# Query projection from SBUF, a reordered query block and paced W2 loads in a one-core transformer layer

## The chip, the core and the metric

The kernel runs on one core of a Trainium2 chip. A core has a matrix engine (PE, with its weight loads listed apart as PEld), a vector engine (DVE), a scalar engine for activations (ACT), a general engine (POOL) and a queue engine that issues the DMA transfers (SP). They run side by side and wait for each other through semaphores. SBUF is the on-chip working memory, PSUM the eight banks that PE writes its sums to, and DRAM the memory off the core. The metric is the device time of one execution in microseconds (us), the median of several runs; less is better.

## The reference

One pre-norm transformer layer on 2048 tokens of width 1024, in bf16: 32 heads of 32 channels, full (not causal) softmax attention, and an MLP of width 3584 with the tanh form of GELU.

```python
def _A_ref(x, wqkv, wo):
    qkv = (x @ wqkv).reshape(B, S, 3, H, Dh).transpose(2, 0, 3, 1, 4)
    q, k, v = qkv[0], qkv[1], qkv[2]
    p = softmax(einsum("bhqd,bhkd->bhqk", q, k) * Dh ** -0.5)
    o = einsum("bhqk,bhkd->bhqd", p, v)
    return o.transpose(0, 2, 1, 3).reshape(B, S, D) @ wo

def _B_ref(x, w1, b1, w2, b2):
    return gelu(x @ w1 + b1) @ w2 + b2          # gelu: tanh form

h  = x + _A_ref(layernorm(x), wqkv, wo)
h2 = h + _B_ref(layernorm(h), w1, b1, w2, b2)
```

## The kernel before, in words

**Tiling.** The 2048 tokens are 16 tiles of 128 (`tt`), four stretches of 512 (`tc`), or eight query blocks of 256 (`qb`, and `u` in the second half of the layer). The 1024 channels are eight groups `g` of four heads. An attention job is one query block and one group: eight rounds, and in each round PE makes the scores of 256 keys for four heads (`qk`, line 796), ACT takes two exponentials of 128 x 1024 (line 807), and PE multiplies them with V (`pv`, line 833) and sums the denominators with a ones matrix (`den`, line 862). There are 64 jobs, and so 1024 exponentials.

**Stages.** At the head, x is loaded, normalised and transposed into `xnT`, four stretches of 512 tokens. Q, K and V of group 0 come first, with the jobs of query blocks 0 to 2 of that group. Then, for g from 1 to 7, `rest_of_projections(g)` makes Q of the first 512 tokens, K of all tokens and V of the next group, and `attention` runs query blocks 0 and 1 of the group (for groups 1 and 2 also block 2). The Q of later tokens goes through DRAM: each result of 128 x 512 is copied out of PSUM by DVE and written to `q_scratch`, and `load_q` fetches 256 columns of it when a job begins. For the second 512 tokens, groups 0, 1 and 2 are projected from `xnT` in SBUF (`proj(0, g, 1, ...)`, through two staging buffers `stg`); the other five groups come later, in `late_q(1, 1, [3..7])`. A `late_q` loads x of its 512 tokens back from a DRAM copy `xd` (1 MB) into one of two buffers `xq`, loads the query weights in blocks of 512 KB into a ring of four, `w1r` (`wblock`), and projects with those. `late_q(2, 0)` and `late_q(3, 1)` do the same for the third and the fourth 512 tokens, for all eight groups.

**Second half.** For a unit `u` of 256 tokens, `wo(u)` is the output projection with the residual, `ln2(u)` the second layer norm followed by two DMA transposes that put the result into `hnT`, `ffn1(u)` 14 blocks of the first MLP matrix, each with a 512 KB load into the ring `w1r`, a bias addition on DVE and, every second block, the tanh on ACT (line 1014), and `ffn2(u, j)` half of the second MLP matrix: seven loads of 512 KB into the ring `w2r` of seven slots, and 56 matmuls of 512 columns. `wo(u)` loads its 2 MB of weights into the same four slots as the ring `w1r`. `wo(u)` needs all eight groups of attention for its query block. The program lists the work as `wo(u+1)`, `ffn2(u,0)`, `ln2(u+1)`, `ffn2(u,1)`, `ffn1(u+1)`, and then attention of query block u+3.

**The order of the work.** Every instruction is a task with its dependencies. `Graph.schedule` (line 109) plans the order for each engine from assumed durations, among them a DMA rate of 280 GB/s with one transfer after the other, and this order is then fixed: an engine waits at the instruction that is next in its list. On PE, `pick_pe` (line 1210) takes `qk` first, `pv` when enough rounds wait, and otherwise the earliest ready piece of the rest, called background here ("bg": projections, `wo`, `ffn1`, `ffn2`). An attention job holds one of the two PSUM banks 6 and 7 while it runs, and background pieces use what is left of these two. SP, the only queue that issues DMAs, takes the ready transfer with the lowest priority number, and of equals the one that the program lists first. A transfer can be given additional tasks that it waits for (`after`).

**Places in SBUF.** The memory of the first half (`ph0`: `xnT` in four stretches of 8 KB per partition, the weight blocks `Wall0`, `1`, `3`, `4`, `5` of 8 KB each, `stg`) is used again in the second half (`ffn`: from its start 8 KB of `hch`; then 18 KB of `gT` and `uu`, with `xq0`, `xq1` and `lq` in the same place; 4 KB of `hnT`; 16 KB of `w1r`; 28 KB of `w2r`; 4 KB). A transfer into the second use waits until the first use has been read for the last time. In the kernel before, `xq0` lies over `xnT` of the second 512 tokens, `xq1` over that of the third, `hch` over the first, and `w1r` over the end of the fourth, `Wall0` and most of `Wall1`.

Of the kernel before, what the change touches and what calls it, by code (L numbers as in the profile page):

```python
# [328 lines left out]
def build_kernel(nc, A_x, A_wqkv, A_wo, B_w1, B_b1, B_w2, B_b2, out):  # L329
# [87 lines left out]
    ffn = Area(top.cur)  # L417


    xnT, B_xnTt = sb(ph0, "xnT", [P, 4, DC, 512], BF, 4, 4)  # L420
    k_hi = Area(B_KT[8 * (G - 2)].lo)
    Wall, B_W = [], []
    for k in range(6):
        h, b = sb(k_hi if k == 2 else ph0, "Wall%d" % k, [P, DC, 512], BF, 1, 4)
        Wall.append(h)
        B_W.append(b)
    assert k_hi.cur <= B_V[0].lo
    NXB = 4
    v_hi = Area(att_hi - 2 * NT * P * 2)
# [225 lines left out]

    def tr_tile(tt, bank, evac, prio=0):
        tc, t4 = divmod(tt, 4)
        transposes(xb[:, tt % NXB, :], B_xb[tt % NXB], bank, xnT[:, tc, :, t4 * P:(t4 + 1) * P], B_xnTt[tc][t4], evac, prio)

    def proj(which, g, tc, bank, evac, direct=False):  # L660

        blk, c = divmod(which * D + g * P, 512)
        o = B_stg[cnt["sg"] % NSG]
        free = o.w + o.r if which == 0 and not direct else []
        for dc in range(DC):
            mm(bank, Wall[blk][:, dc, c:c + P], xnT[:, tc, dc, :], dc == 0, dc == DC - 1,
               [B_W[blk][c // P]] + B_xnTt[tc], True, after=free if dc == 0 else ())
        if which == 1:
            dst, wr = KT[:, g, 512 * tc:512 * tc + 512], B_KT[8 * g + 2 * tc:8 * g + 2 * tc + 2]
        elif direct:  # L670
            n = q_slot(0, g, 2)
            q_slots[1, g] = n + 1
            dst, wr = QT[:, n:n + 2, :].rearrange("p a c -> p (a c)"), B_QT[n:n + 2]
        else:
            s = cnt["sg"] % NSG
            cnt["sg"] += 1
            dst, wr = stg[:, s, :], [B_stg[s]]
        if evac == "act":
            t = act(lambda a: a.activation(dst, psum[:, bi(bank), :], ACT.Copy), 512, reads=[bb(bank)], writes=wr, prio=-1)
        else:  # L680
            t = dve(lambda v: v.tensor_copy(dst, psum[:, bi(bank), :]), c_dve_ps(512), reads=[bb(bank)], writes=wr)
        drop(t, bank)
        if which == 0 and not direct:
            dma(qd[g, tc], dst, P * 1024, reads=wr, writes=[B_qd[g][tc]], prio=0)
# [37 lines left out]
    def proj_v(tt, q, bank, evac, after=()):  # L722
# [3 lines left out]
        for k in range(2):  # L726
            tc, t4 = divmod(tt + k, 4)
            for dc in range(DC):
                mm(bank, xnT[:, tc, dc, t4 * P:(t4 + 1) * P], Wall[blk][:, dc, c:c + 256], dc == 0, dc == DC - 1,
                   B_W[blk][c // P:c // P + 2] + [B_xnTt[tc][t4]], True, cols=(256 * k, 256 * k + 256), after=after)  # L730
        dst = V[:, 2 * q:2 * q + 2, tt:tt + 2, :]
        wr = [B_V[NT * g + tt + k] for g in (2 * q, 2 * q + 1) for k in range(2)]
# [4 lines left out]
    def proj_v1(tt, g, n, bank, evac, c0=0, narrow=False, after=()):  # L737

        for k in range(n):
            tc, t4 = divmod(tt + k, 4)  # L740
            for dc in range(DC):
                mm(bank, xnT[:, tc, dc, t4 * P:(t4 + 1) * P], Wall[4][:, dc, P * g:P * g + P], dc == 0, dc == DC - 1,
                   [B_W[4][g], B_xnTt[tc][t4]], narrow, cols=(c0 + P * k, c0 + P * k + P), after=after)
        dst = V[:, g, tt:tt + n, :]
        wr = [B_V[NT * g + tt + k] for k in range(n)]
# [9 lines left out]
    def proj_half(which, hc, bank, evac):  # L755
# [1 line left out]
        tc, h = divmod(hc, 2)  # L757
        blk = 2 * which
        for dc in range(DC):
            mm(bank, Wall[blk][:, dc, 0:P], xnT[:, tc, dc, 256 * h:256 * h + 256], dc == 0, dc == DC - 1,  # L760
               [B_W[blk][0]] + B_xnTt[tc][2 * h:2 * h + 2], True, cols=(0, 256))
        if which == 1:
            dst, wr = KT[:, 0, 256 * hc:256 * hc + 256], [B_KT[hc]]
# [210 lines left out]
    def ffn1(u, tail=False):  # L974
        R = R2 if tail else R1
        for blk in range(FC // 2):
            s = wblock(R, None, block=blk)
            bank = blk % 6 if tail else slot()
            for f in range(2):
                for dc in range(DC):  # L980
                    mm(bank, R.w1[:, s, dc, f * P:(f + 1) * P], hnT[:, dc, :], dc == 0, dc == DC - 1,
                       [R.B_w1[s]] + B_hnT, not tail, (256 * f, 256 * f + 256))
            evict1(u, 2 * blk, bank, tail)
            if not tail and blk % 2:
                gelu(u, blk // 2)

    biased = []

    def evict1(u, fc, bank, tail):
        g, B_g = gs[u], B_gs[u][fc // 2]  # L990
# [27 lines left out]
    def ffn2(u, j, wide=False, W=None, banks=None):  # L1018
# [3 lines left out]
        ws = []  # L1022
        for q in range(FC // 4):
            s = W.next("w2", W.nw2)
            dma(W.w2[:, s, :, :], w2d[j, q], P * 4096, reads=[B_w2d[j][q]], writes=[W.B_w2[s]], prio=1)
            ws.append(s)
        for t in range(2):
            bank = banks[t] if banks and banks[t] is not None else slot()
# [34 lines left out]
    def lead_norm(hc):  # L1063
# [6 lines left out]
        for tt in tts:  # L1070
            if tt < LEAD_PE:
                tr_tile(tt, slot(), "act" if tt in LEAD_ACT else "dve")
            else:
                tc, t4 = divmod(tt, 4)
                last_t[:] = [dma_transpose(xnT[:, tc, :, t4 * P:(t4 + 1) * P], xb[:, tt % NXB, :], P * 2048, [B_xb[tt % NXB]], [B_xnTt[tc][t4]], -4)]
            if tt + 8 < NT:
                last_x.append(x_tile(tt + 8, -4))
    lead_rounds = []
# [29 lines left out]
    rest_w(WQ, P, 2 * P)  # L1108
    rest_w(WV, P, 4 * P)
    lx = last_t or last_x[-1:]  # L1110
    for tc in range(1, 4):
        dma(xd[tc - 1], xnT[:, tc, :, :], P * 8192, reads=B_xnTt[tc], writes=[B_xd[tc - 1]], prio=1)
    rest_w(WK, 2 * P, 3 * P)
    rest_w(WQ, 2 * P, 3 * P)
    rest_w(WK, 3 * P, 4 * P)
# [37 lines left out]
    for g in range(1, G):  # L1153
# [4 lines left out]
        attention(1, [g])  # L1158
        if g in EXTRA:
            attention(2, [g])  # L1160
    for g in range(1, 2):
        if g not in EXTRA:
            proj(0, g, 1, slot(), "dve")
    block_copies()
    late_q(1, 1, [g for g in range(2, G) if g not in EXTRA])
    wo(0)
    ln2(0)
    late_q(2, 0, range(G))
    late_q(3, 1, range(G))
    ffn1(0)  # L1170
    attention(2, [g for g in range(1, G) if g not in EXTRA])
# [145 lines left out]
```

## Time and profile before

| what | value |
|---|---|
| median of 3 runs | 1081.43 us (1081.03 to 1085.59) |
| the profiled execution's own time | 1080.46 us |
| its span | 1078.7 us |
| ACT busy | 1012.8 us, 94% |
| PE busy | 1041.8 us, 97% |
| DVE busy | 751.5 us, 70% |
| exponentials on ACT | 1024 (992 into `PT`, 32 into `PX`), 924.5 + 31.3 us |
| tanh on ACT | 49, 57.2 us |
| DMA traffic | 196.37 MB, mean 182 GB/s |

Times inside the execution are microseconds from the start of the span. "Busy" is the time in which at least one instruction of the engine runs; matmuls overlap and are counted through their pipeline, so a busy PE is not a PE at its peak. The granted clock (PEclk) is the share of its full rate that the chip let PE run at; 1.00 is full. In a line of the timeline, what stands in brackets is the engine's idle time just before, and what ended it.

### The profile page before, as it was taken

Reading aid. Unit: us, or ns where it says so; the run is one execution under the profiler, and the core shown is the slowest. Engines: PE = TensorE matmul, PEld = TensorE weight load, DVE = VectorE, ACT = ScalarE, POOL = GpSimd, SP = SyncE. Lnnn points to the kernel's source line nnn. Section 1 sums busy time; section 2 is a strip of 40 time slices with the busy share of each in tenths; the row PEclk is TensorE's granted clock in tenths of the full one; section 3 lists DMA queues with packets and bytes.
Section 4 is the critical chain, followed back from the end, with each engine's and each line's share of the span. In section 5 each row is a group of like instructions: output and inputs, shape, how many; then the busy total and the mean of one; then the engine's idle time right before and its main releaser. Section 6 shows DMA issues by size and latency. Waiting matters only on the chain.

```text
span 1078.7 us, 41723 instructions
## 1 busy us (share of the span) xinstructions
PE 1041.8 (97%) x18987; PEld 608.7 (56%) x19044; DVE 751.5 (70%) x1438; ACT 1012.8 (94%) x1116; POOL 43.4 (4%) x110
## 2 busy tenths in 40 slices
PE   8999999998899999999999999999999999899998
PEld 6566555554344754674475457447545744474483
DVE  8766666566586896698499669849966967596401
ACT  4999999999999999999999999999999999999650
POOL 4200000000010001001000100100010001000100
PEclk9999999999899999999999999999999999899999
DMA  8560544438474645744764574476466455866260
GB/s 233 151 184 21 154 137 119 139 119 296 157 188 134 206 172 181 251 167 154 260 221 168 188 247 165 149 258 221 158 210 233 178 192 206 241 230 238 91 242 20
DMA packets 136177, 196.37 MB, mean 182 GB/s; under 512 B 49216, under 2 KB 100288, under 8 KB 133184
## 3 DMA queue, kind: packets, MB, share of 16 engines
q1 hardware_dynamic: 136000, 193.70, 53.8%
q8 instruction: 149, 2.44, 0.9%
q14 instruction: 28, 0.23, 0.1%
HBM read 177.94 MB, written 27.26 MB: 190 GB/s over the span
## 4 chain that ended last, share of the span: by engine, by line
ACT 74%; PE 24%; DVE 2%; issue 1%; POOL 0%; POOLq 0%
ACT PT L807 67%; PE ps L559 6%; PE ps L562 5%; PE ps L556 5%; ACT uu L1014 4%; PE ps L796 3%; ACT PX L807 3%; PE ps L833 2%; PE ps L862 1%; PE ps L1055 1%; DVE PS L848 0%; PE ps L629 0%; ACT xnT L636 0%; DVE hch L957 0%; DVE st L608 0%
## 5 line engine op out<-in xcount | busy, mean ns | idle before, releaser
L807 ACT ACTIVATE PT<-ps 128x1024 bf16<-128x1024 f32 x992 | 924.5, 1116 | 7.4 <-PE ps L796 7.3
L848 DVE TENSOR_TENSOR PS<-PT 128x1024 bf16<-128x1024 bf16 x431 | 286.8, 686 | 125.8 <-ACT PT L807 65.1
L796 PE MATMUL ps<-QT,KT 32*128 32x256 bf16 x4096 | 205.0, 274 | 8.9 <-ACT PT L807 5.7
L833 PE MATMUL ps<-PT,V 128*32 128x256 bf16 x3968 | 175.7, 274 | 3.6 <-ACT PT L807 3.5
L796 PEld LDWEIGHTS ps<-QT,KT 32*128 32x128 bf16 x4096 | 61.0, 92 | 164.6 <-ACT PT L807 145.3
L862 PE MATMUL ps<-PS,ones 128*32 128x256 bf16 x1756 | 122.2, 274 | 3.0 <-DVE PS L848 2.7
L559 PE MATMUL ps<-hnT,a_w1r 128*128 128x256 bf16 x979 | 119.1, 273 | 1.7 <-DVE hch L1037 0.5
L833 PEld LDWEIGHTS ps<-PT,V 128*32 128x32 bf16 x3968 | 101.6, 97 | 33.4 <-ACT PT L807 6.3
L559 PEld LDWEIGHTS ps<-hnT,a_w1r 128*128 128x128 bf16 x979 | 90.1, 98 | 26.7 <-issue 15.7
L556 PE MATMUL ps<-a_w2r,gT 128*32 128x512 bf16 x1380 | 99.8, 381 | 0.4 <-DVE gT L1016 0.3
L559 PE MATMUL ps<-a_w2r,gT 128*128 128x512 bf16 x390 | 96.2, 380 | 2.8 <-issue 1.9
L556 PE MATMUL ps<-hnT,a_w1r 128*32 128x256 bf16 x2356 | 83.4, 276 | 1.4 <-DVE gT L992 1.0
L992 DVE TENSOR_TENSOR gT<-ps,b1f 128x512 bf16<-128x512 f32 x98 | 67.3, 687 | 14.5 <-PE ps L559 8.0
L1037 DVE SCALAR_TENSOR_TENSOR hch<-ps,hch 128x512 bf16<-128x512 f32 x32 | 22.0, 689 | 72.1 <-PE ps L562 47.1
L556 PEld LDWEIGHTS ps<-hnT,a_w1r 128*32 128x32 bf16 x2356 | 58.5, 97 | 15.2 <-issue 11.7
L559 PEld LDWEIGHTS ps<-a_w2r,gT 128*128 128x128 bf16 x411 | 35.3, 98 | 46.9 <-issue 12.5
L862 PEld LDWEIGHTS ps<-PS,ones 128*32 128x32 bf16 x1756 | 46.3, 96 | 25.1 <-DVE PS L848 8.8
L1014 ACT ACTIVATE uu<-uu 128x1024 bf16<-128x1024 bf16 x49 | 57.2, 1168 | 0.0
L559 PE MATMUL ps<-xnT,Wall 128*128 128x512 bf16 (+1 forms) x256 | 54.0, 344 | 2.4 <-issue 1.0
L556 PEld LDWEIGHTS ps<-a_w2r,gT 128*32 128x32 bf16 x1380 | 29.9, 96 | 25.7 <-issue 15.2
L613 POOL CAST mvb<-mv 128x2 bf16<-128x2 f32 (+1 forms) x25 | 5.1, 211 | 976.4 <-DVE mv L610 976.4
L878 DVE STREAM_TRANSPOSE OD<-ps 128x256 f32<-128x256 f32 x64 | 28.6, 447 | 11.5 <-PE ps L833 5.9
(91 smaller groups left out, 1018.4 us busy)
## 6 DMA issues: line engine op xcount, KB each, us to landing
a_w2r<-w_blocks SPq DMA_DIRECT2D x105, 512.0 KB, 5.6
a_w1r<-w_blocks SPq DMA_DIRECT2D x98, 512.0 KB, 3.7
wov<-wo_blocks SPq DMA_DIRECT2D x16, 1024.0 KB, 4.8
w_blocks<-in_B_w_dram SPq DMA_DIRECT2D x28, 512.0 KB, 4.0
b_w1r<-w_blocks SPq DMA_DIRECT2D x14, 512.0 KB, 4.1
a_w1r<-in_A_wqkv_dram SPq DMA_DIRECT2D x11, 512.0 KB, 5.2
Wall<-in_A_wqkv_dram SPq DMA_DIRECT2D x17, 256.0 KB, 4.5
xrb<-in_A_x_dram SPq DMA_DIRECT2D x16, 256.0 KB, 4.7
```

Source lines behind the costliest of these rows:

```text
L556: fns.append(lambda p, j=j: p.matmul(psum[32 * j:32 * j + 32, bi(bank), c0:c1], lhsT[:, 32 * j:32 * j + 32], rhs, start=start, stop=stop, ...
L559: t.whole = lambda p: p.matmul(psum[:, bi(bank), c0:c1], lhsT, rhs, start=start, stop=stop, skip_group_check=True)
L562: t = pe(lambda p: p.matmul(psum[:, bi(bank), c0:c1], lhsT, rhs, start=start, stop=stop), occ, reads=reads, writes=[bb(bank)], mode="full" ...
L796: return p.matmul(psum[:, 2 * us[h // 2] + h % 2, 256 * i:256 * i + 256], KT[32 * h:32 * h + 32, g, k0:k0 + P], QT[32 * h:32 * h + 32, qs, :],
L807: act(lambda a, u=u, k=k: a.activation(PTs[s][:, k, :, :], psum[:, 2 * u:2 * u + 2, :], ACT.Exp, bias=0.0, scale=SCALE), 1024, reads=[B_ps ...
L833: fns.append(lambda p, i=i, h=h: p.matmul(psum[32 * h:32 * h + 32, bi(bank), 0:256], V[:, g, 2 * r + i, 32 * h:32 * h + 32], PTs[s][:, h / ...
L848: dve(lambda v: v.tensor_tensor(PS[:, n, :, :], pairs[:, :, 0:256], pairs[:, :, 256:512], ALU.add), c_dve(1024, 2), reads=B_PTs[s], writes ...
L862: fns.append(lambda p, h=h, rhs=rhs, i=i: p.matmul(psum[32 * h:32 * h + 32, bi(bank), 256:512], ones32[:, :], rhs, start=False, stop=last, ...
L878: t = dve(lambda v: v.transpose(OD[:, o, 1, :], psum[:, bi(bank), 256:512]), 0.36, reads=[self.B_O, self.B_D], writes=B_D, prio=-1)
L992: t = dve(lambda v: v.tensor_tensor(g[:, fc:fc + 2, :], psum[:, bi(bank), :].rearrange("p (f c) -> p f c", f=2), b1f[:, fc:fc + 2].unsquee ...
L1014: act(lambda a: a.activation(w, w, ACT.Tanh, bias=0.0, scale=KT2), 1024, reads=[B_uu[i]], writes=[B_uu[i]], prio=-1)
L1037: drop(dve(lambda v, hs=hs, bank=bank, half=half: v.scalar_tensor_tensor(hch[:, hs, c], psum[:, bi(bank), :], half, hch[:, hs, c], ALU.mul ...
```

## The change

Three things change.

The places in SBUF: `xnT` becomes four tensors, and these and the weight blocks are laid out in the order xnT1, Wall4, xnT0, xnT2, xnT3, Wall3, Wall5, Wall0, Wall1. So xnT1 (the second 512 tokens) lies under `hch`, Wall4 (V of the first four groups) under `xq0`, xnT0 under `xq1`, parts of xnT2, xnT3 and Wall3 under `w1r`, and Wall0 and Wall1 (the query weights) under `w2r`.

The Q work: `late_q(1, 1, [3..7])` is gone. Groups 3 to 7 of the second 512 tokens are projected by `proj(0, g, 1, ...)` from `xnT` and `Wall` in SBUF, after the attention of group 7 in the listing. The DRAM copy of these tokens of x (1 MB) is not written and not read. `late_q(2, 0, range(G))` is listed ahead of `wo(0)` and `ln2(0)`, in place of behind them.

The W2 loads: for j = 0 and u from 0 to 6, load q of `ffn2(u, 0)` waits in addition for the last matmul of block 2q of `ffn1(u)`.

```diff
-    xnT, B_xnTt = sb(ph0, "xnT", [P, 4, DC, 512], BF, 4, 4)
     k_hi = Area(B_KT[8 * (G - 2)].lo)
-    Wall, B_W = [], []
-    for k in range(6):
-        h, b = sb(k_hi if k == 2 else ph0, "Wall%d" % k, [P, DC, 512], BF, 1, 4)
-        Wall.append(h)
-        B_W.append(b)
+    Wall, B_W = [None] * 6, [None] * 6
+    xnT, B_xnTt = [None] * 4, [None] * 4
+    Wall[2], B_W[2] = sb(k_hi, "Wall2", [P, DC, 512], BF, 1, 4)
+    for kind, k in (("x", 1), ("W", 4), ("x", 0), ("x", 2), ("x", 3), ("W", 3), ("W", 5), ("W", 0), ("W", 1)):
+        h, b = sb(ph0, ("xnT%d" if kind == "x" else "Wall%d") % k, [P, DC, 512], BF, 1, 4)
+        if kind == "x":
+            xnT[k], B_xnTt[k] = h, b
+        else:
+            Wall[k], B_W[k] = h, b
...
@@ ffn1
+            blocks1.setdefault(u, []).append(gr.tasks[-1])
             evict1(u, 2 * blk, bank, tail)
...
@@ ffn2
-            dma(W.w2[:, s, :, :], w2d[j, q], P * 4096, reads=[B_w2d[j][q]], writes=[W.B_w2[s]], prio=1)
+            dma(W.w2[:, s, :, :], w2d[j, q], P * 4096, reads=[B_w2d[j][q]], writes=[W.B_w2[s]], prio=1,
+                after=blocks1[u][0 + 2 * q:][:1] if j == 0 and 0 <= u < 7 else ())
...
-    for tc in range(1, 4):
-        dma(xd[tc - 1], xnT[:, tc, :, :], P * 8192, reads=B_xnTt[tc], writes=[B_xd[tc - 1]], prio=1)
+    for tc in range(2, 4):
+        dma(xd[tc - 1], xnT[tc][:, :, :], P * 8192, reads=B_xnTt[tc], writes=[B_xd[tc - 1]], prio=1)
...
-    for g in range(1, 2):
-        if g not in EXTRA:
-            proj(0, g, 1, slot(), "dve")
+    for g in range(3, G):
+        proj(0, g, 1, slot(), "dve")
     block_copies()
-    late_q(1, 1, [g for g in range(2, G) if g not in EXTRA])
+    late_q(2, 0, range(G))
     wo(0)
     ln2(0)
-    late_q(2, 0, range(G))
     late_q(3, 1, range(G))
     ffn1(0)
```

The other lines of the diff only write `xnT[tc][:, ...]` where `xnT[:, tc, ...]` stood.

## The prediction

> **What bounds the kernel now.** I read the page's busy times and slices first, then the chain that ended last, then ACT's timeline for its idle times, and last the table by stretches and the SP queue around these.
>
> ```profile
> PE 1041.8 (97%) x18987; PEld 608.7 (56%) x19044; DVE 751.5 (70%) x1438; ACT 1012.8 (94%) x1116; POOL 43.4 (4%) x110
> ACT  4999999999999999999999999999999999999650
> PEclk9999999999899999999999999999999999899999
> ACT 74%; PE 24%; DVE 2%; issue 1%; POOL 0%; POOLq 0%
> ```
>
> ACT is full from slice 2 to slice 37, and the chain runs over it for 74%. So the time is three pieces: the head to the first exponential at 22.28 us, the exponentials and tanhs to about 1012.2, and the tail to 1078.7, a chain of PE work of the last query block. The change touches neither head nor tail. What it can save is ACT's idle time in the middle, and that is little:
>
> ```profile
> 292.21 11.12 ACT L807 ACTIVATE PT<-ps 128x1024 bf16<-128x1024 f32 x12 [1.55 <-PE ps L796]
> 303.52 16.89 ACT L807 ACTIVATE PT<-ps 128x1024 bf16<-128x1024 f32 x18 [0.19 <-PE ps L796]
> 646.20 2.86 ACT L807 ACTIVATE PT<-ps 128x1024 bf16<-128x1024 f32 x3 [0.47 <-PE ps L796]
> 729.20 8.36 ACT L807 ACTIVATE PT<-ps 128x1024 bf16<-128x1024 f32 x9 [0.22 <-PE ps L796]
> 917.41 2.86 ACT L807 ACTIVATE PT<-ps 128x1024 bf16<-128x1024 f32 x3 [0.37 <-PE ps L796]
> 933.74 8.36 ACT L807 ACTIVATE PT<-ps 128x1024 bf16<-128x1024 f32 x9 [1.50 <-PE ps L796]
> ```
>
> These are all of them: 4.30 us, 0.4% of the time. The two large ones follow stretches in which PE ran short of background. In the table by stretches (first PE, PEld, DVE, ACT and POOL busy; then PEclk, DMA share, GB/s):
>
> ```profile
> 259.00:266.00 7.00, 4.41 (x97) 1.74 (x98) 4.03 (x7) 6.93 (x9) 0.00 (x0) 1.00 0.95 345
> 279.00:289.00 10.00, 6.97 (x153) 3.29 (x154) 5.55 (x12) 10.00 (x12) 0.00 (x0) 0.80 0.81 283
> 289.00:302.00 13.00, 12.98 (x203) 5.88 (x206) 8.45 (x16) 11.45 (x13) 2.23 (x4) 0.89 0.33 96
> 918.00:930.00 12.00, 7.89 (x164) 2.86 (x152) 6.52 (x12) 12.00 (x14) 0.00 (x0) 0.86 0.98 283
> 930.00:934.00 4.00, 4.00 (x84) 2.38 (x80) 0.69 (x1) 2.50 (x4) 0.00 (x0) 0.56 0.23 89
> 1004.00:1011.00 7.00, 4.89 (x117) 2.21 (x110) 3.45 (x6) 6.99 (x8) 0.00 (x0) 1.00 0.10 25
> ```
>
> A lull itself costs ACT nothing, since attention is taken first. It costs when the clock falls (0.80 and 0.86 as means) and the first background burst runs at half rate in front of a score matmul:
>
> ```profile
> 289.02 2.77 PE L559 MATMUL ps<-wov,OT 128*128 128x512 bf16 x6 [0.44 <-DVE OT L893]
> ```
>
> Six matmuls of 512 columns in 2.77 us, where seven take 1.68 us at full clock; ACT's 1.55 us is this. The lulls of 7 us (259 and 1004) left the clock at 1.00.
>
> **Part 1, Q of the second 512 tokens.** Removed: three 512 KB weight blocks, 1 MB of x written and 1 MB read. The 40 matmuls stay, 40 x 0.215 = 8.6 us of PE (0.215 from 54 to 56 matmuls in the tail's 12.03 us), and so do five DVE copies of 0.69 us and five writes of 128 KB. They used to wait for x and weights from 259.9 to 265.9; now both lie in SBUF when K of group 7 ends, near 259, so the 6 us lull goes. It cost ACT nothing (0.07 us busy short), so the gain here is 0; what it gives is that background runs 6 us ahead. Staging: two `stg` buffers, each free when its write has landed (median 3.1 us); behind a project-and-copy of about 3.6 us this can hold a group by 0 to 1.5 us, which the next Q block fills. `hch` now waits for the last of these projections, about 273; it is needed by `wo(0)` at 294 or later.
>
> **Part 2, the third 512 tokens ahead of `wo(0)`.** It moves 64 matmuls (13.8 us of PE), eight copies on DVE, one load of 1 MB, four of 512 KB and eight writes of 128 KB past `wo(0)` (32 matmuls, two loads of 1 MB, two of 256 KB) and past `ln2(0)`, whose POOL work (2.2 us in 289 to 302) and two DMA transposes come later on POOL and SP. Its x can load early, over `Wall4`; its weights wait for K of group 7 and land some 5.2 us behind it, under the Q work. Background gets 0.63 of PE beside attention (8.6 us in 265.9 to 279.6). So it runs from 259 to 259 + 22.4/0.63 = 295, and the lull from 279.6 to 289.0, in which PE waited for the attention output of group 7, is filled. The stall of 1.55 us and the 0.19 us behind it go: -1.74 us (bounds: 0, if a wait of the same size takes its place, since `wo(0)` now waits for its second megabyte, 4.8 us behind the last Q matmul, with 16 matmuls on the first megabyte as cover; and -1.74). `wo(0)` ends near 310 instead of 302.7. Behind it stands the fourth Q block, 13.8/0.63 = 22 us, which hides `ln2(0)` and its transposes.
>
> Together background is about 15 us ahead at `ffn1(0)` (335 instead of 349.8). The units then come every 94.8 us (the loads of `wo` at 383.8, 478.5, 573.2, 668.3, 763.3), against 126 us of exponentials and tanhs each, so background stays bound by PE until it catches up with attention, and that is at unit 6: its last attention output is written at 892.4, and `wo(6)` starts at 892.7.
>
> **Part 3, the W2 loads.** Nothing less is loaded. The seven loads of `ffn2(u,0)` leave the end of `ffn2(u-1,1)` and go out with every second block of `ffn1(u)`, each behind the W1 load that the same matmul frees. Load 6 goes out one block (2.4 us) before `ffn1` ends and lands in 5.6 us; it is read 24 matmuls into `ffn2(u,0)`, 8 us on: hidden. On SP a waiting W2 load holds what is queued behind it, Q loads for attention and W1 loads. At unit 6 it matters most:
>
> ```profile
> 907.92 3.35 SPq L580 DMA_DIRECT2D a_w2r<-w_blocks  x4
> 911.31 3.60 SPq L585 DMA_TRANSPOSE hnT<-a_xb  x1
> 916.56 2.80 SPq L585 DMA_TRANSPOSE hnT<-a_xb  x1
> ```
>
> The transposes go out behind four W2 loads, take 8.7 us to land where those of unit 1 took 2.9, and `ffn1(6)` starts only at 930.2. Without the loads they land about 6 us sooner. But the 12 us of `ffn2(5,1)` that ran behind `wo(6)`, from 906 to 918, will by then be done, for background is 15 us ahead. So the lull stays, from about 902 to 912 instead of 918 to 930, and I leave its 1.50 us where they are (bounds -1.50, and +0.24 by the other such stall, 1.74). The 0.37 us at 917 fell into the load burst and goes; 0.47 and 0.22 us stand 13 and 5 us behind such bursts (622 to 633, 718 to 728), and I take half: together -0.37 - 0.35 = -0.72 us (bounds -1.06, and +1.06 should the loads beside W1 disturb as much as the bursts did).
>
> **What is late next.** If `ffn1(6)` starts 18 us sooner, background ends 18 us sooner, at 986 instead of 1004; the half of `ffn2(6,1)` kept for the tail is bound to a bank that attention holds. Then 986 to 1011 is attention alone, the longest lull of all, and the tail starts at half clock. Recovery took 2.7 us from 289.0 and 3.4 us from 930.2; half of such a stretch of dense PE work is 1.4 to 1.7 us. I take +1.5 (bounds 0, if the clock holds, and +3.4, if twice as long).
>
> Sum: -1.74 - 0.72 + 0 + 1.5 = -0.96 us, on the profiled execution's own 1080.46: 1079.5. The median of the runs lies 0.97 above that execution; I forecast **1079.5 us** and let the range carry that difference.
>
> The Trainium skill, "TensorE: Matmul & The Clock Gate", section "HAM oscillation", puts it as no PE gap above some 3.4 us. By that rule no lull here would throttle: attention never leaves PE idle for more than 1.42 us. The trace disagrees (0.80 and 0.86 with gaps of at most 1.42 us), so I keep the 1.5 us; by the rule the sum would be 1078.0.
>
> **Rivals.**
> *The clock holds in the last lull*, as in those of 259 and 1004; PE's share in 918 to 930, where it fell, speaks against. Then the 1.5 us are not paid: 1080.46 - 1.74 - 0.72 = 1078.0, and 1076.5 if unit 6 also loses its stall, the transposes being early enough.
> *Filled lulls come back with interest.* Both stalls of 1.5 to 1.7 us return at other places (at `wo(0)`'s second megabyte, at unit 6) and the tail pays up to 3.4: 1080.46 - 0.72 + 3.4 = 1083.1, about 1084 on the median.
> *W1 comes late, the other side.* Block k + 4 of `ffn1` is asked for when block k ends and read three blocks on, 3 x 2.4 = 7.1 us. It lands in 3.9 us now, at most 7.1. With W2 between, 21 loads of 512 KB in 34 us make 324 GB/s, under the 419 that 705 to 710 reached. If W1's landing passes 8.0 us (7.1, and the 0.9 us of one exponential that is queued), PE stands in front of score matmuls; at 8.3, the most a W2 load took, 0.3 us x 7 blocks x 7 units = 15 us: 1095. At 8.1 it would be 5 us, 1085.
> *It does nothing*: other work shows at the same places, 1080.5 to 1081.5.
>
> **How the numbers follow.** Forecast (1078.5 to 1081) 0.45; the clock holds 0.22; with interest 0.20; W1 late 0.10; nothing 0.03. More than 0.5% (5.4 us), about what a measurement of this kernel can tell from no change, would have to come from 4.3 us of idle time: faster 0.04. Slower, above 1086.8, is most of the late W1: 0.09. Same 0.87. The range goes from 1080.46 - 1.74 - 1.06 - 1.50 = 1076.2 to the second rival's 1084 and the 1 us between medians, 1085; it leaves out most of the late W1 and the lowest edge, 0.13.
>
> **What would show it.** Right: no `lq` copies before 272, ACT not idle in 280 to 305, PE at 1.00 there; `ffn1(0)` near 335; no W2 load before `ffn1(0)`; a lull at 902 to 912 with an ACT stall at its end; attention alone before 1011 and matmuls of the tail at half rate. Wrong: ACT idle at many places inside `ffn1`, W1 landing above 7 us, or a last exponential that ends after 1013.

## The result, and the profile after

The changed kernel takes 1094.12 us (median, 1091.68 to 1097.2) where the kernel before, run beside it, took 1082.08 us (1079.89 to 1085.59): 1.0115 times the time, 95% interval 1.0089 to 1.0140. The change costs 12 us; the forecast was 1 us of gain and a range that ended at 1085. The profiled execution took 1096.74 us, its span is 1094.6 us (before 1078.7).

From the page of the changed kernel, the busy times, two rows of the slices and the chain that ended last:

```profile
PE 1047.4 (96%) x19009; PEld 609.6 (56%) x19068; DVE 748.5 (68%) x1438; ACT 1015.9 (93%) x1116; POOL 46.9 (4%) x110
ACT  4999999999999999999999999999999999999650
PEclk9999999999999999999999999999999998899799
ACT 52%; PE 40%; DVE 4%; issue 2%; POOL 1%; DMA 0%; SPq 0%; POOLq 0%; DVEq 0%
```

The coarse rows look as before, ACT full from slice 2 to 37. The chain does not: ACT carries 52% of it instead of 74%, PE 40% instead of 24%, and "issue", time in which the engine waited for nothing that the profile shows, has gone from 1% to 2%.

The span splits at the first exponential that is written to `PT` and at the last one (two into `PX` run earlier, before at 15.5 and 17.3 us, so what the prediction calls the first exponential is the first into `PT`):

| piece | before, us | after, us | difference |
|---|---|---|---|
| head, to the first exponential into `PT` | 22.28 | 21.90 | -0.4 |
| from there to the last exponential | 989.9 | 1004.0 | +14.1 |
| tail | 66.5 | 68.8 | +2.3 |

In the middle piece ACT was idle for 4.30 us before and for 15.11 us after, 10.8 us more. The other 3.3 us are ACT's busy time, which rose by 3.1 us over the whole execution. Part of them goes with the number of gaps, 21 against 6: exponentials that follow each other without a gap start some 0.92 us apart, and one that runs alone takes 1.02 (the row of 539.79 below), so each gap also loses an overlap of about 0.1 us, 1.5 us for 15 more gaps. The rest is not accounted for. The largest, from ACT's timeline of the changed kernel (start, length, what ran, in brackets the idle time before it):

```profile
378.48 3.08 ACT L810 ACTIVATE PT<-ps 128x1024 bf16<-128x1024 f32 x3 [1.45 <-PE ps L799]
539.79 1.02 ACT L810 ACTIVATE PT<-ps 128x1024 bf16<-128x1024 f32 x1 [1.22 <-PE ps L799]
558.79 1.94 ACT L810 ACTIVATE PT<-ps 128x1024 bf16<-128x1024 f32 x2 [1.39 <-PE ps L799]
640.43 1.94 ACT L810 ACTIVATE PT<-ps 128x1024 bf16<-128x1024 f32 x2 [0.73 <-PE ps L799]
837.39 4.74 ACT L810 ACTIVATE PT<-ps 128x1024 bf16<-128x1024 f32 x5 [0.79 <-PE ps L799]
935.43 1.94 ACT L810 ACTIVATE PT<-ps 128x1024 bf16<-128x1024 f32 x2 [1.62 <-PE ps L799]
```

All wait for score matmuls (line 799, line 796 before). The stalls of 1.55 and 0.19 us at 292 and 303 are gone: ACT is never idle between 280 and 345. In their place stand 17 gaps between 348 and 838, 12.3 us together; 15 of them, 11.5 us, lie in stretches in which `ffn1` runs, the other two (at 577 and 709) outside. The table by stretches shows the places that the prediction spoke of (first PE, PEld, DVE, ACT and POOL busy; then PEclk, DMA share, GB/s):

```profile
280.00:290.00 10.00, 9.84 (x209) 4.97 (x209) 7.83 (x15) 10.00 (x11) 0.00 (x0) 1.00 0.73 242
920.00:930.00 10.00, 7.18 (x108) 2.09 (x104) 6.90 (x14) 9.54 (x11) 2.68 (x4) 0.64 1.04 244
930.00:940.00 10.00, 8.88 (x92) 5.55 (x96) 4.90 (x10) 7.97 (x10) 0.00 (x0) 0.68 0.46 165
1005.00:1010.00 5.00, 3.65 (x90) 1.76 (x86) 2.68 (x4) 5.00 (x7) 0.00 (x0) 1.00 0.18 51
1010.00:1026.00 16.00, 10.47 (x166) 3.64 (x160) 6.38 (x12) 15.53 (x17) 0.00 (x0) 0.65 0.13 48
```

The lull of 280 to 289 is filled at full clock, as intended. The lull of unit 6 is still there, at 919 to 931. And the lull at the end that the prediction feared is there too: attention alone, PE busy for 10.47 of 16 us and the clock at 0.65.

**What a gap looks like on PE.** From PE's timeline of the changed kernel, the two groups around one of them:

```profile
555.29 0.72 PE L559 MATMUL ps<-hnT,a_w1r 128*32 128x256 bf16 x18
557.25 0.29 PE L559 MATMUL ps<-hnT,a_w1r 128*32 128x256 bf16 x2 [1.23 <-issue]
```

Line 559 is the matmul of FFN1 as column tiles: one product of 128 x 128 weights is four instructions of 32 columns each, on the same data. PE did 18 of a piece of 20, stopped for 1.23 us, and did the other two. A late load of W1 would stop it ahead of a group of four, where its data is first needed, not after the second of four; and the profile has no wait here, only "issue". The table by stretches, cut at eight such stops (the counts in brackets are instructions):

```profile
377.83:442.87 65.04, 63.20 (x1143) 31.70 (x1149) 43.86 (x85) 64.26 (x70) 3.42 (x8) 1.00 0.49 161
442.87:461.57 18.70, 17.51 (x381) 12.88 (x381) 17.33 (x33) 18.02 (x20) 0.00 (x0) 1.00 0.80 280
461.57:538.68 77.11, 74.27 (x1396) 40.06 (x1403) 54.43 (x107) 75.99 (x83) 3.18 (x8) 1.00 0.52 178
538.68:557.25 18.57, 17.34 (x381) 12.93 (x382) 15.60 (x30) 17.46 (x19) 0.00 (x0) 1.00 0.77 257
557.25:639.54 82.29, 78.47 (x1523) 43.41 (x1530) 58.62 (x113) 80.41 (x88) 3.18 (x8) 1.00 0.52 179
639.54:737.70 98.16, 93.35 (x1778) 54.49 (x1782) 73.92 (x141) 94.95 (x104) 3.41 (x8) 1.00 0.58 191
737.70:833.12 95.42, 93.10 (x1778) 54.46 (x1781) 73.22 (x141) 94.27 (x103) 3.77 (x8) 1.00 0.59 198
```

Matmuls and weight loads together are 2292, 762, 2799, 763, 3053, 3560 and 3559. These are 9, 3, 11, 3, 12, 14 and 14 times some 254. So PE stops where a fixed number of instructions ends, whatever they do. The page has a row that fits, the DMA queue that brings instructions (packets, MB, share of 16 engines):

```profile
q8 instruction: 149, 2.44, 0.9%
```

2.44 MB in 149 packets are 16.4 KB each, and PE's 19009 + 19068 instructions in blocks of 254 are 150 blocks. In the trace's records of single DMA packets, one packet of this queue starts shortly before PE goes on, in each of the eight:

| PE goes on, us | the packet started, us | lead, us | packets since the row above |
|---|---|---|---|
| 377.83 | 375.60 | 2.2 | |
| 442.87 | 440.53 | 2.3 | 9 |
| 461.57 | 459.37 | 2.2 | 3 |
| 538.68 | 536.51 | 2.2 | 11 |
| 557.25 | 555.00 | 2.3 | 3 |
| 639.54 | 637.15 | 2.4 | 12 |
| 737.70 | 735.28 | 2.4 | 14 |
| 833.12 | 830.70 | 2.4 | 14 |

The packets between two stops number exactly 9, 3, 11, 3, 12, 14 and 14. Numbered this way, the packet for a block starts 5.1 us (median) before PE enters the block, and in the kernel before 5.5. Leads under 2.6 us, between 300 and 1000 us, number some 18 after and some 6 before; some instructions are missing from the trace, so away from the stops these numbers are rough. Counted back 254 instructions from each of the eight, PE had entered the block that it was using 2.6 to 3.4 us before the packet for the next one started; over all blocks this is some 1.0 to 1.5 us. So the packets of the eight started late.

In all, PE of the changed kernel has eleven stops above 0.35 us marked "issue" between 60 and 1030 us, 10.8 us together, and each of the eleven ends 2.2 to 2.5 us behind the start of a packet. The kernel before has two such stops, 1.1 us. Of ACT's 15.1 us of idle time, 10.3 us stand at most 4.3 us behind one of them. The rest is 2.5 us at the lull of unit 6, and 2.3 us that no such stop explains.

This gives the reading that the experiments test, called the fetch (theory F): PE's own instructions come by DMA, one block ahead. Where PE uses up a block quickly while bulk loads fill the DMA engines, the next block starts late and PE stands. The Trainium skill, "Runtime: NRT & Kernel Launch", section "Instruction fetch mechanics", describes blocks of 16 KiB, 256 instructions, loaded while the one before executes, and calls the crossing "mostly hidden"; the packets here agree in size and count, the stops of 1 us disagree with the last. The rivals: W1 comes late (the prediction's); paced loads hold up what is queued behind them on SP; or the new order of the work costs something that has nothing to do with DMA.

### The profile page after: what moved, and what is told of

Its sections match the earlier page's. It is cut to its first block, busy times and chain, and to the rows that moved or that the text cites. A ratio compares the mean times of both kernels' runs of the same rounds, so it can differ in the third digit from the quotient of the medians.

```text
span 1094.6 us, 41732 instructions
## 1 busy us (share of the span) xinstructions
PE 1047.4 (96%) x19009; PEld 609.6 (56%) x19068; DVE 748.5 (68%) x1438; ACT 1015.9 (93%) x1116; POOL 46.9 (4%) x110
## 3 DMA queue, kind: packets, MB, share of 16 engines
q8 instruction: 149, 2.44, 0.9%
## 4 chain that ended last, share of the span: by engine, by line
ACT 52%; PE 40%; DVE 4%; issue 2%; POOL 1%; DMA 0%; SPq 0%; POOLq 0%; DVEq 0%
ACT PT L810 47%; PE ps L562 13%; PE ps L559 9%; PE ps L799 6%; PE ps L565 5%; PE ps L836 4%; PE ps L865 3%; ACT PX L810 3%; ACT uu L1019 2%; DVE PS L851 1%; DVE st L611 1%; DMA xrb<-in_A_x_dram 0%; DVE OD L881 0%; DVE hch L960 0%; DVE uu L1018 0%
## 5 line engine op out<-in xcount | busy, mean ns | idle before, releaser
L799 PE MATMUL ps<-QT,KT 32*128 32x256 bf16 x4096 | 206.0, 275 | 10.1 <-ACT PT L810 7.8
L562 PE MATMUL ps<-a_w2r,gT 128*128 128x512 bf16 x371 | 91.4, 380 | 4.7 <-issue 3.5
L559 PE MATMUL ps<-hnT,a_w1r 128*32 128x256 bf16 x2428 | 88.6, 274 | 6.7 <-issue 4.1
L562 PE MATMUL ps<-xnT,Wall 128*128 128x512 bf16 (+1 forms) x290 | 62.3, 348 | 2.5 <-issue 1.1
L865 PEld LDWEIGHTS ps<-PS,ones 128*32 128x32 bf16 x1756 | 47.2, 97 | 30.1 <-issue 10.5
L562 PEld LDWEIGHTS ps<-a_w2r,gT 128*128 128x128 bf16 x398 | 34.1, 98 | 46.5 <-issue 13.1
L1019 ACT ACTIVATE uu<-uu 128x1024 bf16<-128x1024 bf16 x49 | 52.8, 1083 | 0.0
L559 PEld LDWEIGHTS ps<-a_w2r,gT 128*32 128x32 bf16 x1432 | 31.7, 96 | 27.0 <-issue 14.1
```

Source lines behind the costliest of these rows:

```text
L559: fns.append(lambda p, j=j: p.matmul(psum[32 * j:32 * j + 32, bi(bank), c0:c1], lhsT[:, 32 * j:32 * j + 32], rhs, start=start, stop=stop, ...
L562: t.whole = lambda p: p.matmul(psum[:, bi(bank), c0:c1], lhsT, rhs, start=start, stop=stop, skip_group_check=True)
L799: return p.matmul(psum[:, 2 * us[h // 2] + h % 2, 256 * i:256 * i + 256], KT[32 * h:32 * h + 32, g, k0:k0 + P], QT[32 * h:32 * h + 32, qs, :],
L865: fns.append(lambda p, h=h, rhs=rhs, i=i: p.matmul(psum[32 * h:32 * h + 32, bi(bank), 256:512], ones32[:, :], rhs, start=False, stop=last, ...
L1019: act(lambda a: a.activation(w, w, ACT.Tanh, bias=0.0, scale=KT2), 1024, reads=[B_uu[i]], writes=[B_uu[i]], prio=-1)
```

## The experiments

Each stands against runs of the kernel before on the same chip (medians 1084.18 us for the first four, 1083.31 for the next four, 1083.38 for the last four). In the order of the argument:

| kernel | median, us | ratio to before | 95% interval |
|---|---|---|---|
| part 3 alone (e1) | 1090.29 | 1.0059 | 1.0032 to 1.0086 |
| parts 1 and 2, not 3 (e2) | 1089.91 | 1.0052 | 1.0038 to 1.0066 |
| part 1 alone (e10) | 1090.51 | 1.0055 | 1.0033 to 1.0078 |
| part 2 alone (e11) | 1090.80 | 1.0055 | 1.0035 to 1.0074 |
| before + copies of 512 KB (e4) | 1103.55 | 1.0180 | 1.0147 to 1.0213 |
| before + copies of 4 KB (e7) | 1084.15 | 1.0002 | 0.9982 to 1.0023 |
| changed, FFN1 not tiled (e3) | 1078.25 | 0.9947 | 0.9929 to 0.9966 |
| before, FFN1 not tiled (e5) | 1080.01 | 0.9965 | 0.9945 to 0.9986 |
| parts 1 and 2, FFN1 not tiled (e6) | 1081.58 | 0.9972 | 0.9951 to 0.9992 |
| e2, block ends moved (e9) | 1090.72 | 1.0059 | 1.0040 to 1.0079 |
| e3 + filler in the last lull (e8) | 1076.17 | 0.9939 | 0.9914 to 0.9964 |
| e8, FFN2 not tiled either (e12) | 1086.99 | 1.0034 | 1.0017 to 1.0051 |

### The parts: pacing alone (e1), and everything but the pacing (e2)

e1 is the kernel before with only this:

```diff
+            blocks1.setdefault(u, []).append(gr.tasks[-1])
...
-            dma(W.w2[:, s, :, :], w2d[j, q], P * 4096, reads=[B_w2d[j][q]], writes=[W.B_w2[s]], prio=1)
+            dma(W.w2[:, s, :, :], w2d[j, q], P * 4096, reads=[B_w2d[j][q]], writes=[W.B_w2[s]], prio=1,
+                after=blocks1[u][0 + 2 * q:][:1] if j == 0 and 0 <= u < 7 else ())
```

> Only the W2 pacing, on the kernel before. Theory F (the W2 loads put beside FFN1 delay the fetch of PE's own instructions, which FFN1 uses up fastest, so PE stands still in the middle of matmul groups and ACT runs dry): 1090 to 1097 us, PE breaks above 0.5 us marked issue inside FFN1 as in the changed kernel. Rival L (the loss comes from background running ahead of attention, parts 1 and 2): 1080 to 1083 us, no such breaks.

e2 is the changed kernel with the W2 load back as it was.

> Parts 1 and 2 without the W2 pacing. F: 1078 to 1083 us, the stall at 292 us gone, ACT idle in the FFN1 stretches under 1.5 us in all. L: 1090 us or more. On both, a lull behind wo(6) and one before the last exponential, with the clock down, if background really runs some 15 us ahead.

Pacing alone costs 0.59%, the rest alone 0.52%, and together they make 1.11%, the measured 1.15% within the intervals. So neither is the only cause. ACT's idle time is 13.1 us in e1 and 12.8 us in e2. e1 lies at the edge of what theory F was taken to give. e2 does not: 1078 to 1083 was expected of F, and 1089.91 is the number of its rival L, background that runs ahead. The time alone thus speaks for both causes, one for each half; the traces show the same stop on PE in both. PE's timeline of e1:

```profile
457.91 0.51 PE L556 MATMUL ps<-hnT,a_w1r 128*32 128x256 bf16 x10
459.60 0.72 PE L556 MATMUL ps<-hnT,a_w1r 128*32 128x256 bf16 x18 [1.18 <-issue]
```

And of e2:

```profile
538.56 0.39 PE L559 MATMUL ps<-hnT,a_w1r 128*32 128x256 bf16 x6
539.70 0.72 PE L559 MATMUL ps<-hnT,a_w1r 128*32 128x256 bf16 x18 [0.76 <-issue]
```

Ten and six are no multiples of four: in the middle of a product again. The instruction packets started 2.5 and 2.4 us before 459.60 and 539.70.

What parts 1 and 2 move is FFN1 against the load burst of W2, which the expectation for e2 had left out. The stretch of the W2 burst in the kernel before, in the table by stretches:

```profile
533.70:537.90 4.20, 4.20 (x108) 2.25 (x100) 2.24 (x4) 4.20 (x5) 0.00 (x0) 1.00 1.03 392
```

The same in e2:

```profile
535.50:538.60 3.10, 3.10 (x108) 2.34 (x103) 2.25 (x4) 3.10 (x4) 0.00 (x0) 1.00 1.01 377
```

And in the changed kernel, a block in which the loads of W1 and the paced loads of W2 run together:

```profile
551.90:555.10 3.20, 3.20 (x116) 2.49 (x106) 2.96 (x6) 3.20 (x4) 0.00 (x0) 1.00 0.91 309
```

By these rows both halves are needed, dense instructions and full DMA engines; the copies and the untiled FFN1 below test one each. Before, the burst had the DMA engines full (1.03), but PE ran matmuls of 512 columns of FFN2 and took 4.2 us for 108 of them; no stop followed. In e2 PE ran tiles of 256 columns under the burst, 108 in 3.1 us, and stopped at 538.6. In the changed kernel the pacing itself puts the loads there.

### Part 1 alone (e10) and part 2 alone (e11)

e10 is the kernel before with the new places in SBUF and Q of the second 512 tokens from SBUF; e11 is the kernel before with `late_q(2, 0, range(G))` ahead of `wo(0)`:

```diff
+    late_q(2, 0, range(G))
     wo(0)
     ln2(0)
-    late_q(2, 0, range(G))
```

> Part 1 alone: Q of the second 512 tokens from SBUF and the new layout; late_q(2) behind wo(0) as before, no pacing. If the order of parts 1 and 2 matters only through where block ends fall, this can come out anywhere from 1082 to 1091, with breaks marked issue accounting for the ACT idle above 4 us. The stall at 292 us stays, since PE still waits for the attention output of group 7 there.

> Part 2 alone: late_q(2) ahead of wo(0) on the kernel before, no new layout, no pacing. The stall at 292 us goes (-1.7 us); the rest as in the run of part 1: 1080 to 1089, by the breaks.

Each costs 0.55% alone, as much as both together in e2. ACT was idle for 15.2 us in e10 and 13.0 us in e11. The 1090.80 us of e11 are above the 1089 that was expected at most. Not all of this idle time is the fetch: 9.2 us in e10 and 5.9 us in e11 stand at most 6 us behind a stop marked "issue". In e10 3.9 us fall between 279 and 306, where the first Q burst runs at half rate (six matmuls of 512 columns in 2.77 us) and the Q work waits 0.50 us for its staging and 1.31 us for its weights; the stall at 292 us did not stay, as had been expected. In e11 one gap alone is 5.42 us, on ACT's timeline:

```profile
446.87 5.61 ACT L807 ACTIVATE PT<-ps 128x1024 bf16<-128x1024 f32 x6 [5.42 <-PE ps L833]
```

PE's timeline of e11 through it:

```profile
441.12 5.36 PE L556 MATMUL ps<-a_w2r,gT 128*32 128x512 bf16 x96
446.42 0.62 PE L833 MATMUL ps<-PT,V 128*32 128x256 bf16 x16
```

PE lacks nothing here: it runs 96 matmuls of FFN2 in one piece, and the products with V, which ACT waits for, stand behind them in the fixed order. Why the plan put them there was not tried. So the half percent of each part alone mixes stops of the fetch with such accidents of the order, and it is not split further here.

### Traffic that nobody waits for: large copies (e4) and small ones (e7)

e4 is the kernel before with one more DMA behind every second block of `ffn1`, a copy of a block of W2 to a place in DRAM that nobody reads. No engine waits for the copies; only SP issues them. The planner counts them, though, so that PE's order is that of before only up to 468 us of the kernel before, and then shifts.

```diff
+            if u < 7 and blk % 2 == 0:
+                extra(u, blk // 2, gr.tasks[-1])
...
+    xtra = nc.dram_tensor("xtra", [49, P, 4, 512], BF, kind="Internal").ap()
+
+    def extra(u, q, t):
+        dma(xtra[7 * u + q], w2d[0, q], P * 4096, reads=[B_w2d[0][q]], prio=1, after=[t])
```

> The kernel before, with seven copies of 512 KB from DRAM to DRAM beside each FFN1 (units 0 to 6), issued behind every second block as the paced loads are; nothing ever waits for their data, and W2 stays where it was. F: the same kind of breaks at instruction blocks, slower by 4 to 15 us (1086 to 1097). W2 arriving late as the cause: no change, 1080 to 1083 us.

In e7 each copy takes 4 KB instead of 512 KB, so that SP's queue is held in the same way and the DMA engines are not. PE's order is that of before throughout.

```diff
-        dma(xtra[7 * u + q], w2d[0, q], P * 4096, reads=[B_w2d[0][q]], prio=1, after=[t])
+        dma(xtra[7 * u + q][:, 0, 0:16], w2d[0, q][:, 0, 0:16], P * 32, reads=[B_w2d[0][q]], prio=1, after=[t])
```

> As the run with copies beside FFN1, but each copy moves 4 KB in place of 512 KB: the same waits stand in the SP queue in front of the same loads, without the traffic. F: as the kernel before within 3 us, no breaks above 0.7 us in FFN1. If holding the SP queue were the cause: slower by 8 to 20 us as with the big copies.

The large copies cost 19 us, more than the 4 to 15 expected, the small ones nothing (1.0002). The held queue is out as a cause of a loss of this size; e7 still has three stops above 0.35 us (2.2 us together, the one in FFN1 0.95 us, more than expected). In e4 19.9 us of idle time on ACT stand against 4.3, in gaps of up to 2.9 us.

How much of the 19 us is the shifted order is not separated, but where the order is still the same the traffic alone shows its price. At the group that the kernel before starts at 358.1 us e4 is 1.1 us behind, at that of 468.1 us it is 6.2 us behind. Between them e4 has four stops marked "issue", 5.2 us together, and the kernel before none. PE's timeline of e4 at the first:

```profile
363.28 0.49 PE L556 MATMUL ps<-hnT,a_w1r 128*32 128x256 bf16 x9
364.90 0.62 PE L556 MATMUL ps<-hnT,a_w1r 128*32 128x256 bf16 x15 [1.13 <-issue]
```

The same 24 instructions in the kernel before:

```profile
362.18 0.83 PE L556 MATMUL ps<-hnT,a_w1r 128*32 128x256 bf16 x24
```

Later PE's timeline of e4 shows the longest stop of all, and not in FFN1:

```profile
575.02 0.27 PE L833 MATMUL ps<-PT,V 128*32 128x256 bf16 x2
577.56 0.61 PE L833 MATMUL ps<-PT,V 128*32 128x256 bf16 x6 [2.27 <-issue]
```

Line 833 multiplies exponentials with V: both operands are in SBUF, no DMA brings them, and two of the eight had already run. A late weight load cannot stop these. The instruction packet started 2.2 us before 577.56. This speaks as clearly as any line against "W1 late".

### Fewer instructions: FFN1 without column tiles (e3, e5, e6)

In the changed kernel the product of FFN1 is made by one instruction of 128 columns instead of four of 32; the same numbers are computed, the loads are the same.

```diff
-                       [R.B_w1[s]] + B_hnT, not tail, (256 * f, 256 * f + 256))
+                       [R.B_w1[s]] + B_hnT, False, (256 * f, 256 * f + 256))
```

> The changed kernel, with every matmul of FFN1 (units 0 to 6) as one instruction of 128 columns instead of four of 32: a quarter of the instructions for the same work and the same loads; more switches between tilings. F: the breaks marked issue inside FFN1 go, ACT idle there falls from 12 to under 3 us, 1080 to 1086 us. Rival W (PE waits for W1 data that land late, or for what SP holds back): the stops stay, 1091 to 1097 us.

The loss is gone and more: 1078.25 us, 0.9947 of before, against 1.0115 for the changed kernel, and below the 1080 to 1086 expected. ACT is idle for 1.24 us in all (15.11), and PE has no stop above 0.35 us marked "issue". The gaps at the lull of unit 6, 2.5 us, are gone as well, which is the order and not the fetch. The instruction queue on its page:

```profile
q8 instruction: 135, 2.21, 0.8%
```

14 blocks fewer. The table by stretches of e3 has the loads as dense as ever, without a stop:

```profile
445.00:450.00 5.00, 5.00 (x57) 3.77 (x55) 4.42 (x8) 5.00 (x6) 0.00 (x0) 1.00 0.93 324
```

DMA share 0.93, and PE busy for all of the 5 us, but with 57 matmuls in them, 57/5.0 = 11 per us where the block before the stop at 555.9 had 116/3.2 = 36. The products are the same; what is less is how fast instructions are used up. (The planner lays out the rest of PE's work somewhat differently too.) Leads under 2.6 us are some 2 instead of some 18.

The same edit on the kernel before (e5) and on parts 1 and 2 (e6) asks what is left of the change once the fetch is out of the way:

> The kernel before, with the matmuls of FFN1 (units 0 to 6) as one instruction each. Theory F (fetch of PE's instructions): the kernel before has only two small stops of this kind (0.47 and 0.22 us), so about 0 to -2 us (1081 to 1085 beside 1084 for the kernel before); the stall at 292 us stays. If instead one instruction for four saves PE time in itself, -4 us or more.

> Parts 1 and 2 without the pacing, FFN1 as one instruction each. F: the breaks of 0.7 to 1.8 us of the run without pacing go, and the time falls by 6 to 10 us, to 1078 to 1083. If it lies beside the paced kernel with the same FFN1 (1078), the pacing neither helps nor hurts once the instructions are few.

e5 is 0.9965 of before, 3.3 us less, where 0 to -2 was expected of F and -4 or more of an instruction that is cheaper in itself. ACT is idle for 1.88 instead of 4.30 us, but little of that is the fetch: behind such stops stand 0.59 us of it in e5 and 0.69 us before, and what went are the gaps of unit 6 (1.87 us), with the order. So untiling is not a clean cure of the fetch alone. Against e5, the changed kernel without tiles (e3) is 0.9947/0.9965 = 0.998, and parts 1 and 2 alone (e6) are 1.0007; neither can be told from 1 by intervals of 0.002 on each. The profiled executions of e3 and e5 differ by 1078.71 - 1079.62 = -0.9 us, but the executions of one kernel lie up to 5 us apart. So with few instructions the change is worth about nothing; the gain of 1 us that was forecast is neither shown nor ruled out. The 12 us go where instructions are few, and most of their idle time stands behind stops of the fetch.

### Does it matter where the block ends fall? (e9)

e2 with eight score steps near the start issued twice: 128 PE instructions more, half a block, so all later block ends move by half a block against the work.

```diff
+        again = [t for t in self.seqs[E.PE] if t.kind == "qk"][30:38]
...
-            for fn in t.fns:
+            for fn in t.fns * (2 if t in again else 1):
```

> Parts 1 and 2 without the pacing, with eight score steps near the start issued twice (same values written twice), which moves every later instruction of PE by 128, half a block of instructions, and changes nothing else in the order. Theory F: the breaks move to where the new block ends meet loads; by the trace of the run without the shift, block ends at 538, 635 and 731 us would no longer meet both a full DMA and a dense stretch, those at 438 and 830 still would. ACT idle from 400 to 860 us falls from 11 to about 4 us, and the time from 1090 to 1082 to 1087. If the breaks belong to the work and not to the blocks: same places, 1090.

By its time this expectation missed: I held it likely that the shift would take block ends out of the bursts. It is 1.0059 where e2 was 1.0052, and stops stand at 443, 541, 636 and 829 us, near those of e2 (443, 540, 638, 832). Both are what the expectation named for breaks that belong to the work. The counts of instructions say otherwise. From the start to just before the stop near 443 us, in the table by stretches, first e2 and then e9:

```profile
0.00:443.33 443.33, 426.84 (x7970) 248.24 (x8000) 307.52 (x594) 428.13 (x466) 25.26 (x62) 1.00 0.53 160
0.00:443.06 443.06, 425.72 (x7971) 248.42 (x8000) 304.67 (x587) 425.43 (x462) 25.17 (x62) 1.00 0.52 158
```

Matmuls and weight loads together are 15970 and 15971, though e9 has 128 more of them near the start. So PE stops at the same number of instructions and 128 earlier in the work: in e2 behind two matmuls of FFN1, in e9 behind seven of eight score matmuls. The same holds for the stops near 139 us (4774 and 4776), 638 and 636 us (22834 and 22835), and 832 and 829 us (29698 and 29699). The one near 540 us comes a block later in e9, and the one that e2 has at 733 us is gone; ACT is idle for 10.5 instead of 12.8 us. So the stops follow the count, as F says, and half a block of shift hardly changes the time. A reason would be that a burst and the dense work beside it last longer than a block, so that some end always lies in them; that is argued, not shown.

### The last lull (e8), and the same for FFN2 (e12)

e8 is e3 with 28 matmuls behind `ffn2(6, 0)` whose result nobody uses, to keep PE busy while attention runs alone at the end.

```diff
+    last6 = [t for t in gr.tasks if t.eng == E.PE][-1:]
+    for k in range(7):
+        bank = slot()
+        for i in range(4):
+            mm(bank, ident[:, :], b2t[:, 0:512], i == 0, i == 3, [B_ident, B_b2t], False, after=last6 if i == 0 else ())
+        drop(dve(lambda v, bank=bank: v.tensor_copy(lq[:, 0, 0:8], psum[:, bi(bank), 0:8]), 0.15,
+                 reads=[bb(bank)], writes=[B_lq[0]]), bank)
```

> The changed kernel with FFN1 as one instruction each, and 28 matmuls of the identity with a bias row, whose result nothing uses, on PE where it is short of work behind the second half of FFN2 of unit 6. If the cold clock costs the tail: the clock stays at 1.00 up to the tail, the time from the last exponential to the end falls from 68.9 to about 66.5 us, and the median to 1075 to 1077 us. If the clock is not what makes the tail longer: 1078, no change.

The end of e3 in the table by stretches:

```profile
985.00:1008.10 23.10, 17.63 (x328) 7.51 (x322) 9.55 (x17) 22.72 (x25) 0.00 (x0) 0.85 0.22 77
1008.10:1025.00 16.90, 16.68 (x98) 7.28 (x96) 7.34 (x18) 4.90 (x8) 3.45 (x8) 0.91 0.35 121
```

The end of e8:

```profile
985.00:1008.00 23.00, 22.29 (x367) 9.83 (x365) 10.21 (x24) 22.12 (x25) 0.00 (x0) 1.00 0.23 81
1008.00:1025.00 17.00, 16.76 (x108) 8.87 (x101) 7.99 (x18) 6.83 (x10) 3.45 (x8) 1.00 0.48 167
```

With PE busy the clock stays at 1.00, and the tail is 67.1 us instead of 68.9. e8 is the fastest kernel of this study, 1076.17 us, 0.9939 of before; its lead over e3 (0.9947) lies within the intervals.

e12 is e8 with FFN2 in one instruction as well.

```diff
-                   [B_gs[u][fc // 2], W.B_w2[s]], not wd, after=biased[u:u + 1] if fc == 0 else ())
+                   [B_gs[u][fc // 2], W.B_w2[s]], False, after=biased[u:u + 1] if fc == 0 else ())
```

> The changed kernel with FFN1 and FFN2 as one instruction for each matmul, and the 28 filling matmuls. F: no breaks are left to remove, so no gain beyond the version with FFN1 alone (1076); each switch between attention's tiling and the full one costs PE time, 1075 to 1079.

It is slower, 1.0034 and 1086.99 us where 1075 to 1079 was expected, and not through the fetch: ACT is idle for 0.5 us and ends at 1007.3 as in e8 (1007.1). The tail is 77.3 instead of 67.1 us. PE's timeline of e12 in it:

```profile
1026.66 6.21 PE L565 MATMUL ps<-b2t,ident 128*128 128x512 bf16 x28
```

The planned order came out otherwise: the 28 filler matmuls run in the tail, 6.2 us, and 46 matmuls of FFN2 with them instead of 28, 18 x 0.215 = 3.9 us. Together 10.1 us, nearly the whole difference. What untiled FFN2 is worth by itself is left open.

## Why the prediction was wrong, point by point

**The failing step is Part 3's "-0.72 us (bounds -1.06, and +1.06 should the loads beside W1 disturb as much as the bursts did)".** Measured, the gaps in the FFN1 stretches are 11.5 us of ACT's idle time, and pacing alone costs 0.59%, 6 us. PE stops at the ends of its instruction blocks there, where the next block's packet starts late. The bounds were set by stalls that stood near bursts in the kernel before, where PE ran few, long matmuls under the loads; the step did not count PE itself as a user of the DMA engines. The signs were there: a queue "instruction" with 149 packets on the page, and two gaps, at 646 and 729, whose instruction packets had leads of 2.9 and 2.3 us. The 0.22 us at 729 stand 1 us behind the burst that the prediction lists (718 to 728), not 5.

**"W1 comes late, the other side" had the place and the sign, not the mechanism.** W1 landed in 4.2 us at the median and 7.6 at most, under the 8.0 us from which the rival decided, and the price was paid anyway, with stops in the middle of products and, in e4, in work that needs no load; none of PE's waits in the changed kernel's trace ends on a DMA. That its price, 1095, lies 1 us from the 1094.12 measured is luck. The signs of being wrong that the prediction named did come: ACT idle at many places inside `ffn1`, W1 above 7 us at its most, and a last exponential that ends at 1025.9.

**Parts 1 and 2: the removed waits were right, "What is late next" was not complete.** The stalls at 292 and 303 are gone (-1.74, as predicted), PE is busy for 9.84 of 10 us at 280 to 290, and `ffn1(0)` begins at 334.2 (predicted 335; before 349.8). `lq` copies begin at 265.7, not behind 272, because the third Q block is mixed with the second; the matmuls of `wo(0)` run from 298 to 309 (predicted end 310). What failed is that a lead of 15 us was taken as free. It moves FFN1 under the W2 burst, and e2 pays 0.52%, of which 10.2 of ACT's 12.8 us of idle time stand behind stops of the fetch.

**"The units then come every 94.8 us" failed with it.** The loads of `wo` lie at 370.9, 469.6, 567.5, 665.3, 762.1 and 858.7: 96.6 to 98.7 us apart. The stops eat the lead, so at unit 6 it is gone: `wo(6)` starts at about 906 (predicted 892.7), the lull is at 919 to 931 (predicted 902 to 912, before 918 to 930), and its gaps are 2.48 us (before 1.87).

**The end was right.** Attention alone before 1025, and a tail 2.3 us longer (predicted +1.5, bounds 0 and 3.4). The cleanest sign of the cause is e7, where PE's order is that of before: its clock falls ahead of the tail, and the tail is 68.9 us instead of 66.5. The first 5 us of the tail, before and then e7:

```profile
1012.20:1017.20 5.00, 5.00 (x38) 2.18 (x37) 1.69 (x5) 1.04 (x3) 0.00 (x0) 1.00 0.06 25
1014.90:1019.90 5.00, 5.00 (x33) 1.83 (x30) 1.59 (x5) 0.38 (x1) 0.00 (x0) 0.64 0.14 58
```

At 0.64 these 5 us lose 1.8 us of PE work, most of the 2.5. e8 fits: with PE kept busy the clock holds and the tail is short. The clock is not all that sets the tail, though: e5 has 68.6 us at a clock of 1.00, with another order. The rule of the Trainium skill, "TensorE: Matmul & The Clock Gate", section "HAM oscillation", names gaps of PE above some 3.4 us and, read as the prediction read it, would have left this out; the clock of 0.65 in 1010 to 1026, with no gap above 1.22 us, disagrees once more.

**The sum without the failing step is not contradicted.** With FFN1 untiled on both sides, the change measures about -2 us by the medians' ratios, not distinguishable from zero; the forecast was -0.96. The order changes with the untiling, so this is no test of the single terms.

## What to carry to other kernels

Before loads are moved beside other work, look at how fast the engines there use up instructions: where PE ran 36 matmuls per us with DMA at 0.9 and more, its next instructions came late, and loads as dense beside 11 per us stopped nothing. Stops marked "issue" in the middle of a piece, a whole number of instruction blocks apart, are the sign, and what helped here was fewer, larger instructions. An engine that is brought ahead of its plan is not free either: ask beside which transfers its work now falls.

## What was not expected of the hardware

- PE stops of 0.4 to 2.3 us at ends of blocks of some 254 recorded instructions, 16.4 KB each, when the packet of the next block starts only 2.2 to 2.5 us before; the usual lead was 5.1 to 5.5 us. Where 128 instructions were added ahead, the stops stayed at the same count of instructions.
- DMA traffic alone, with nobody waiting for its data, cost some 5 us in 110 us of the same work in the same order (e4 against before, 358 to 468 us); with the order that shifts behind it 49 copies of 512 KB made the kernel 1.8% slower, while 49 copies of 4 KB at the same places cost 0.02%, which is nothing that these runs can tell.
- With one instruction of 128 columns in place of four column tiles of 32, the kernel before took 0.35% less and the changed one some 1.7% less (ratios to before of 1.0115 and 0.9947), though PE's matmul work is the same; PE's order changed with it.
- With attention alone and PE busy for 73% of 1005 to 1010, the clock was still 1.00; in the 16 us behind it, at 65%, it was 0.65. How long a lull the clock bears was not measured.
